# A list-scheduled attention and MLP kernel on one core: a recalibrated scheduler, other buffers and casts, and a new order of all engines

## The chip, the cores and the metric

The kernel runs on one core of a Trainium2 chip. The core has five engines with an instruction queue each: PE (TensorE, products; its weight loads are shown apart as PEld), DVE (VectorE), ACT (ScalarE), POOL (GpSimd) and SP (SyncE, which here only issues DMAs). Sixteen DMA engines move data between HBM and SBUF. The metric is the device time of one execution in microseconds. Each engine runs its own instructions strictly in their order; between engines, semaphores hold an instruction until what it needs is there.

## What is computed

Linear attention with positive features on 8 batches x 8 heads x 576 positions x 64 channels, then a layer norm and a two-layer MLP with a residual.

```python
def phi(x):                                        # 64 -> 256 features
    proj = np.einsum('bhsd,df->bhsf', x, w_phi)    # w_phi: 64 x 128
    proj = proj - np.max(np.abs(proj), axis=-1, keepdims=True)
    return np.concatenate([np.exp(proj), np.exp(-proj)], axis=-1)
q_p, k_p = phi(q), phi(k)
kv = np.einsum('bhsf,bhsd->bhfd', k_p, v); z = np.sum(k_p, axis=2)
attn = einsum(q_p, kv) / (einsum(q_p, z) + 1e-06)  # then heads joined: x is 8 x 576 x 512
xn = (x - mu) / np.sqrt(var + 1e-06) * g_ln
out = x + np.maximum(xn @ w_ch1, 0.0) @ w_ch2      # 512 -> 2048 -> 512
```

All inputs and the output are float32 in HBM.

## The kernel before

**Units and pairs.** The attention is cut into 32 units of 1152 rows, numbered n = 0 to 31. In pair 0 (units 0 to 7) a unit is two heads of one batch; in pairs 1 to 3 it is one head of two batches. Eight units make a pair, which is two whole batches, that is 9 tiles of 128 rows of `x`. A unit has eight full tiles of 128 rows and one mixed tile of the two leftovers of 64 rows.

**What a unit does.** `load_main` and `load_tails` bring k, q and v (the tails are `qx` and `vx`). q and k are turned so that channels lie on partitions: on PE for units 0 to 7 (`a_trans`, L470 and L478, copied out at L485 and L487), and by DMA from unit 8 on (`a_trans_dma`: two casts to bfloat16, a small one of 128 columns for the tails and a large one of 1024, at L536 on DVE, L538 on ACT or L540 on POOL; then one DMA transpose at L559 on SP's queue). PE makes the projections (L580, L581, L622, L628, L637), DVE the maxima (L584, L686), ACT the exponentials (L593, L597, L700, L754), POOL scales v by them (L712, L717, L721). PE sums over rows into `n_bank` (`a_kv`, L778 and L783), the result is copied to `KV` (L791 or L793), PE multiplies it by the query features (`a_num`, L829 and L835), DVE adds and inverts (L853, L859, L863), POOL puts the quotient into `x` (L869).

**What a pair does.** Once `x` is there, DVE takes statistics (L982, L996), DVE or ACT centers (L1000, L1005), and rows of 384 are turned into `xT` (on PE for pair 0, L946, by DMA for the others). For each of three blocks of 384 rows `moe` makes 16 groups of four products with w_ch1 (L1055, 128x384) and a relu (L1063, L1065), then 3 x 16 products with w_ch2 (L1122, 128x512; the last tile in halves, L1087), the scaled residual (L1130, L1135, L1141) and the store.

**Weights.** w_ch1 and w_ch2 are loaded in four quarters each from POOL's queue, with a cast to bfloat16 (L424, L435). w_ch1 is scaled by g_ln on DVE once pair 1 begins (L450, 16 instructions).

**What sets the order.** The whole order is made when the program is built. Each piece of work is an `Op` with an engine (or several, of which the first free one takes it), an assumed duration, what it reads and writes, and what buffers it acquires. `Order.run` walks through assumed time: each engine that is free takes the ready operation of lowest rank. The rank is the latest start that the end would allow, plus an offset from `OFF` by kind of work and by a table number (`stage_table`); `DUE` and `BLOCK` give the MLP's products due times. DMAs are modelled by two queues, `DMA` and `DMA_w` (those of POOL). A filler is a product of zeros into an unused part of `n_bank` (L1317, L1320); it is put on PE where PE has only operations that lack a buffer, up to the assumed time `WARM`. What `run` gives is emitted as a fixed order on each of the five engines; the assumed times themselves leave no wait behind, only the order does. Dependencies given as `came` (the gates of the weights) act in the assumed time alone.

```python
            late = min((latest[o.number] for o in op.users), default=1000.0) - op.lag
...
                if free[engine] > now + 1e-9 or not queue:
                    continue
...
                    if engine == self.filler[0] and now < self.filler[1]:
                        op = self.fill(now)
```

Of the kernel before, what the change touches and what calls it, by code (L numbers as in the profile page):

```python
# [10 lines left out]
FP32 = mybir.dt.float32  # L11
# [6 lines left out]
def bcast(ap: bass.AP, dim: int, n: int) -> bass.AP:  # L18
# [13 lines left out]
OFF = (  # L32
    {
        "load": 291.2, "trans": 30.0, "trans.copy": 30.0, "mixed": 49.3, "mixed.max": 23.2,
        "mixed.exp": 41.8, "k": 19.6, "k.max": 21.4, "k.em": -15.4, "k.exp": -46.8, "en": 15.6,
        "vv": -27.5, "q": 30.1, "q.max": 47.4, "q.em": 15.6, "tails": -42.2, "tails.exp": 7.3,
        "kv": -52.7, "kv.copy": 4.2, "num0": 51.4, "num1": -54.2, "num.dve": 32.4, "g1": 0.0,
        "g2": 0.0, "g3": 0.0, "put": -53.0, "ln": 201.7, "w1": -144.2, "w2": 207.3,
    },
    {  # L40
        "load": -11.5, "trans": -36.9, "trans.copy": 204.6, "mixed": 25.2, "mixed.max": -80.9,
        "mixed.exp": 132.7, "k": -79.5, "k.max": 146.3, "k.em": 53.6, "k.exp": -36.9,
# [4 lines left out]
    },  # L47
    {
        "load": 22.6, "trans": 17.7, "trans.copy": 96.2, "mixed": -96.6, "mixed.max": -70.2,
        "mixed.exp": -34.7, "k": -33.5, "k.max": -145.4, "k.em": -34.3, "k.exp": -84.1,  # L50
# [8 lines left out]
class Op:  # L59
    __slots__ = (  # L60
        "engines", "engine", "us", "emit", "rank", "lag", "deps", "users", "acquire", "release",
        "ready", "left", "number", "due",
# [9 lines left out]

class Order:


    def __init__(self, room):
        self.ops, self.wrote, self.read, self.room = [], {}, {}, dict(room)
        self.filler = (None, 0.0, 0.0, None)

    def add(self, engine, us, rank, emit, r=(), w=(), acquire=None, release=None, lag=0.2, due=None):  # L80
# [3 lines left out]
        op.engine, op.emit, op.rank, op.lag = None, emit, rank, lag  # L84
        op.acquire, op.release, op.due = acquire, release, due
# [14 lines left out]
    def fill(self, now):  # L100
        op = Op()
        op.engines, op.us, op.emit, op.rank = self.filler[:1], self.filler[2:3], self.filler[3], 0
        op.engine, op.lag, op.acquire, op.release = None, 0.0, None, None
        op.number, op.users, op.ready, op.left = -1, [], now, 0
        return op

    def run(self):
        waiting, free, room, events, done = {}, {}, self.room, [], []
        moving = {"DMA": 0.0, "DMA_w": 0.0}
# [19 lines left out]
        while events:  # L129
# [10 lines left out]
            for engine, queue in waiting.items():  # L140
                if free[engine] > now + 1e-9 or not queue:
                    continue
                passed = []
# [12 lines left out]
                if op is None:  # L156
                    if engine == self.filler[0] and now < self.filler[1]:
                        op = self.fill(now)
                    else:
                        continue  # L160
                op.engine = engine
# [3 lines left out]
                if isinstance(us, Move):  # L165
                    other = "DMA_w" if engine == "DMA" else "DMA"
                    moving[engine] = us.ns
                    turn = moving[other] + TURN if free.get(other, 0.0) > now else 0.0
                    us = us.packets * (us.ns + turn)
                elif isinstance(us, Op):  # L170
                    us = 1.1 if us.engine == "ACT" else 0.0
                end = now + us
# [19 lines left out]
def kernel(  # L192
# [37 lines left out]
    QB = 3  # L230
# [18 lines left out]
    nc.scalar.dma_start(out=wphi_f[D : 2 * D, :], in_=w_phi)  # L249
# [17 lines left out]

    wbk = consts.tile([P, 2, F], BF16, name="wbk")
    nc.vector.memset(wbk, 0.0)
    for i in range(2):  # L270
        rows = slice(i * D, (i + 1) * D)
# [8 lines left out]

    qk_bufs, v_bufs, vx_bufs = [], [], []
    for i in range(NBUF):
        qk_bufs.append(consts.tile([P, 2, HG, MX * D], FP32, name=f"qk{i}"))
        v_bufs.append(consts.tile([P, HG, MX * D], FP32, name=f"v{i}"))
    for i in range(2):

        vx = consts.tile([P, TG, 2, D1], FP32, name=f"vx{i}")
        nc.vector.memset(vx, 0.0)
        nc.vector.memset(vx[0:64, :, 0, D:D1], 1.0)
        nc.vector.memset(vx[64:128, :, 1, D:D1], 1.0)  # L290
        vx_bufs.append(vx)


    ea_bufs = []
    for i in range(2):
        eb = consts.tile([P, 2, (MX + 2) * P], BF16, name=f"ea{i}")
        nc.vector.memset(eb[:, :, MX * P :], 0.0)
        ea_bufs.append(eb)

    w1_sb = consts.tile([P, KC, DH], BF16, name="w1")  # L300
    w2_sb = consts.tile([P, JC, DM], BF16, name="w2")

# [7 lines left out]
    b16_bufs = [consts.tile([P, ST], BF16, name=f"b16_{i}") for i in range(2)]  # L310

# [1046 lines left out]
```

## Time and profile before

| what | value |
|---|---|
| time, median of 3 runs | 386.41 us (382.26, 386.41, 387.24) |
| the profiled execution | 381.13 us, span 379.3 us, granted clock 1.00 |
| busy of the span | PE 95%, DVE 67%, ACT 68%, POOL 54% |
| DMA | 53.31 MB, mean 141 GB/s; HBM read 36.77 MB, written 9.44 MB |
| chain that ended last | PE 62%, DVE 18%, DMA 8%, issue 5% |

The profile's times are of one execution, from its first to its last instruction; the time of a run holds a little more than that span. PE's busy time is the union of its instructions, each with its latency in the array, so an instruction can be shown at 326 ns where its successors follow every 162 ns. The chain of work that ended last cuts each piece to the time in which nothing else was waited for. "Idle before" names the instruction or DMA whose semaphore came last. In the slices each digit is the busy share of a fortieth of the span in tenths.

### The profile page before, as it was taken

To read this page: it belongs to the slowest core of one execution; us is meant where nothing else is said; L and a number is where in the kernel's file an instruction comes from. 1 tells how busy PE (TensorE), PEld (TensorE's weight loads), DVE (VectorE), ACT (ScalarE), POOL (GpSimd) and SP (SyncE) were. 2 spreads that over 40 slices of the span, in tenths; PEclk is the share of its full clock that TensorE was granted. 3 is DMA by queue.
4 is the path that set the end of the run, shared out by engine and by line. 5 is a ranking of instruction groups with operands and counts; after the bars stand their busy time and mean duration, and the time that the engine had idled before them with its cause. 6 is when DMAs were issued, how large, how long until landed. Compare 5 with 4: busy or idle time off the path is not lost.

```text
span 379.3 us, 9487 instructions
## 1 busy us (share of the span) xinstructions
PE 358.9 (95%) x3626; PEld 220.2 (58%) x3626; DVE 254.8 (67%) x557; ACT 257.9 (68%) x574; POOL 204.4 (54%) x350
## 2 busy tenths in 40 slices
PE   4999979988999999999999999999999999999995
PEld 2988856554656555556566555556565555555543
DVE  3698998988999999987787999787749000000001
ACT  3877898968787876896877878786746534444420
POOL 4787878847785768463967835572562101111031
PEclk9999999999999999999999999999999999999999
DMA  8999699999975499956664274430104230101012
GB/s 223 274 223 279 182 225 214 200 276 248 259 203 181 84 229 178 238 108 202 151 167 128 65 158 139 90 61 7 51 13 89 76 88 29 28 30 54 30 55 84
DMA packets 91133, 53.31 MB, mean 141 GB/s; under 512 B 57488, under 2 KB 86544, under 8 KB 91088
## 3 DMA queue, kind: packets, MB, share of 16 engines
q1 hardware_dynamic: 86000, 47.66, 50.5%
q0 software_dynamic: 4384, 4.46, 7.6%
q10 hardware_dynamic: 704, 0.59, 0.6%
q8 instruction: 28, 0.46, 0.5%
q14 instruction: 17, 0.14, 0.1%
HBM read 36.77 MB, written 9.44 MB: 122 GB/s over the span
## 4 chain that ended last, share of the span: by engine, by line
PE 62%; DVE 18%; DMA 8%; issue 5%; POOL 2%; ACT 2%; SPq 1%; DVEq 0%; POOLq 0%; ACTq 0%
PE hT_ps L1055 25%; PE ch_ps L1122 24%; DVE m L686 5%; DMA qkT<-b 5%; DMA qx<-in_k_dram 3%; PE n_bank L783 2%; DVE st L982 2%; PE pm L628 2%; DVE numc L853 2%; DVE numc L859 2%; PE num L829 2%; DMA xT<-xc 1%; DVE hT L1063 1%; PE pt L637 1%; ACT eb L700 1%
## 5 line engine op out<-in xcount | busy, mean ns | idle before, releaser
L1055 PE MATMUL hT_ps<-xT,w 128*128 128x384 bf16 x768 | 152.1, 326 | 1.9 <-DMA xT<-xc 0.8
L1122 PE MATMUL ch_ps<-w,hT 128*128 128x512 bf16 x560 | 150.2, 379 | 0.1
L1055 PEld LDWEIGHTS <-w 128*128 128x128 bf16 x768 | 71.8, 98 | 59.2 <-issue 4.0
L1065 ACT ACTIVATE hT<-hT_ps 128x384 bf16<-128x384 f32 x120 | 59.1, 492 | 56.9 <-PE hT_ps L1055 56.3
L686 DVE TENSOR_REDUCE m<-pm 128x8 f32<-128x1024 f32 x64 | 76.8, 1212 | 13.9 <-PE pm L628 9.7
L869 POOL TENSOR_TENSOR x<-numc,rden 128x384 bf16<-128x384 f32 (+3 forms) x88 | 45.9, 537 | 55.4 <-DVE rden L863 53.6
L1122 PEld LDWEIGHTS <-hT 128*128 128x128 bf16 x560 | 50.8, 98 | 41.4 <-issue 1.6
L700 ACT ACTIVATE eb<-pm 128x1024 bf16<-128x1024 f32 x64 | 65.1, 1038 | 6.3 <-DVE m L686 6.3
L754 ACT ACTIVATE ea<-pt 128x1024 bf16<-128x1024 f32 x64 | 63.6, 1029 | 5.9 <-PE pt L637 5.5
L1141 POOL TENSOR_TENSOR o<-o,x 128x512 f32<-128x512 f32 x20 | 23.1, 1155 | 75.4 <-ACT o L1135 75.4
L1130 DVE SCALAR_TENSOR_TENSOR o<-ch_ps,rstd,x 128x512 f32<-128x512 f32 x15 | 11.1, 741 | 56.7 <-PE ch_ps L1122 56.6
L712 POOL TENSOR_TENSOR vv<-v,em 128x512 bf16<-128x512 f32 x32 | 34.0, 1062 | 20.3 <-issue 15.9
L1063 DVE TENSOR_SCALAR hT<-hT_ps 128x384 bf16<-128x384 f32 x72 | 39.0, 547 | 8.1 <-PE hT_ps L1055 7.7
L712 POOL TENSOR_TENSOR vv<-v,en 128x512 bf16<-128x512 f32 x32 | 34.0, 1062 | 0.0
L829 PEld LDWEIGHTS <-ea 128*128 128x128 bf16 x512 | 23.6, 97 | 9.9 <-issue 3.1
L783 PE MATMUL n_bank<-vv,eb 128*128 128x65 bf16 x512 | 26.9, 194 | 0.0
L540 POOL TENSOR_TENSOR b<-qk,one 128x1024 bf16<-128x1024 f32 x11 | 20.8, 1895 | 10.4 <-DMA qkT<-b 7.2
L783 PEld LDWEIGHTS <-eb 128*128 128x128 bf16 x512 | 22.3, 98 | 3.7 <-issue 0.3
L982 DVE BATCH_NORM_STATS2 st<-x 128x6 f32<-128x512 bf16 (+1 forms) x44 | 24.4, 580 | 0.0
L853 DVE TENSOR_TENSOR numc<-num,em 128x390 f32<-128x390 f32 (+1 forms) x40 | 20.4, 517 | 5.6 <-PE num L829 3.9
L1320 PE MATMUL n_bank<-wz 128*128 128x120 bf16 x333 | 23.0, 221 | 1.2 <-DVE KV L791 0.8
L829 PE MATMUL num<-KV,ea 128*128 128x65 bf16 x416 | 19.7, 193 | 2.0 <-ACT xT L958 0.9
(91 smaller groups left out, 460.3 us busy)
## 6 DMA issues: line engine op xcount, KB each, us to landing
qk<-in_k_dram SPq DMA_DIRECT2D x32, 256.0 KB, 4.3
v<-in_v_dram SPq DMA_DIRECT2D x32, 256.0 KB, 5.6
out_dram<-o SPq DMA_DIRECT2D x31, 256.0 KB, 2.4
qk<-in_q_dram SPq DMA_DIRECT2D x30, 256.0 KB, 5.8
w<-in_moe_w_ch_dram POOLq DMA_DIRECT2D x8, 512.0 KB, 11.1
out_dram<-o SPq DMA_DIRECT2D x10, 128.0 KB, 2.4
qx<-in_k_dram SPq DMA_DIRECT2D x16, 64.0 KB, 4.8
qx<-in_q_dram SPq DMA_DIRECT2D x14, 64.0 KB, 3.5
```

Of the source, the lines that this page charges most:

```text
L686: nc.vector.reduce_max(out=m, in_=ps, axis=AX.X, apply_absolute_value=True)
L700: nc.scalar.activation(eb, ps, AF.Exp, scale=(1.0, -1.0)[t])
L712: nc.gpsimd.tensor_tensor(out=u["vv"][:, t, 0:MX, 0:D], in0=vb[:, hh, :].rearrange("p (c d) -> p c d", d=D), in1=bcast(e[:, 0:MX], 2, D), ...
L754: nc.scalar.activation(u["EA"][:, t, 0:1024], u["pt"], AF.Exp, scale=(1.0, -1.0)[t])
L783: nc.tensor.matmul(ps[:, t, c // 4, :], EB[:, t, c, :], vv[:, t, c, :], start=False, stop=(t == 0 and c == MX - 1), skip_group_check=True,)
L829: nc.tensor.matmul(ps[t][:, i, :], ea(u, t, c), KV[:, t, c // 4, :], start=True, stop=True,)
L869: nc.gpsimd.tensor_tensor(out=dst, in0=st["numc"][ps_, i : i + n, 0:D], in1=bcast(st["rden"][ps_, i : i + n], 2, D), op=ALU.mult,)
L982: nc.vector.bn_stats(out=pr["st"][:, t, half or 0, :], in_=x[:, t, h0 * D : h1 * D])
L1055: nc.tensor.matmul(st["ps"], w1_sb[:, kc, jj * P : (jj + 1) * P], xT_bufs[(pair * NR + r) % XB][:, kc::KC, :], start=(kc == 0), stop=(kc = ...
L1063: nc.vector.tensor_relu(h_sb, st["ps"])
L1065: nc.scalar.activation(h_sb, st["ps"], AF.Relu)
L1122: nc.tensor.matmul(ch[t], hT[r, jj][:, rt * P : (rt + 1) * P], w2_sb[:, jj, :], start=(jj == 0), stop=(jj == JC - 1),)
```

## The change

- **The scheduler's model.** A cast on DVE can be a `Port`: it also waits, in assumed time, for what POOL is doing (`port`), and POOL waits for it. DMA transposes take a `Turn` on SP that grows with what is queued. Lags and durations are set anew (`SLACK`, `LAND`, `LAND_T`, `LAND_W`); the first `COLD` us count PE as 1.9 times slower. The offsets `OFF` have ten tables instead of three: one for each of units 0 to 7, one for units 8 to 15, one for the rest. `DUE` and `BLOCK` change.
- **Fillers.** PE is filled also when no operation at all is ready, up to `WARM` = 75 instead of 45, and `FIRST` = 28 fillers stand ahead of everything. The zeros are written first of all on DVE.
- **Transposes.** Three units ahead instead of two (`AHEAD`), with four `qkT` buffers (`QB`) and three `b16` (`NB16`) instead of three and two.
- **Casts.** The small cast on DVE becomes a `tensor_reduce` with max over single elements. Of the large casts DVE has 10 instead of 4, ACT 5 instead of 9, POOL 9 instead of 11. Of the small ones DVE keeps 8, ACT has 9 instead of 7, POOL 7 instead of 9.
- **Weights.** The gates of w_ch1's quarters are loads of v of units 4 to 6 instead of k and v of unit 3; w_ch2 may follow w_ch1's second quarter instead of its last. On POOL's queue this gives w_ch1's quarters 1 and 2, then 0, w_ch2's quarters 3, 0, 1 and 2, then w_ch1's quarter 3. The loads of units 8 to 15 get a true semaphore wait for w_ch2's quarter 3 (`wait_for_w2`); it stands at the first of them on SP, and what follows on SP stands behind it.
- **Engines.** 8 of the 16 scalings of w_ch1 go to ACT, 2 of the centerings to POOL (`CENTER`); half of w_phi is loaded from POOL's queue instead of ACT's, and its copies go from POOL to DVE.
- `FOLD`, with its new branches (`folded`, `subtract`, `put_heads`, `put_row`), is 0: none of that code is in the program but one constant, `nident`.

The products on PE are the same in number and shape in both programs, but for the fillers: 334 and 614. In the diff the line numbers are those of each file.

```diff
-DUE = 30.89
-BLOCK = 115.16
-WARM = 45.0
-X_DMA, QK_DMA = 1, 8
+DUE = 27.47
+BLOCK = 17.68
+WARM = 75.0
+COLD, FIRST = 5.6, 28
+SLACK = ((0.22, 0.0, 0.0, 1.02), (0.35, 0.6, 1.6, 1.03))
+HOLD = 3
+X_DMA, QK_DMA, AHEAD = 1, 8, 3
-LAND, TURN = 1.7, 0.013
-GATE = (("k", 3), ("k", 3), ("v", 3), ("v", 3))
+FOLD = 0
+LAND, LAND_T, LAND_W, TURN, BARRIER = 2.8, 1.5, 3.0, 0.004, 0.4
+GATE = (("v", 4), ("v", 5), ("v", 5), ("v", 6))
...
+CENTER = ((("DVE", "ACT", "POOL"), (Port(0.27), 0.61, 1.2)), (("DVE", "ACT"), (Port(0.27), 0.61)))
...
-                if free[engine] > now + 1e-9 or not queue:
+                filling = engine == self.filler[0] and now < self.filler[1]
+                if free[engine] > now + 1e-9 or not (queue or filling):
                     continue
...
+                elif isinstance(us, Port):
+                    first, last = port[0], port[1]
+                    us = us.us + max(0.0, first - now if now < first else last - now)
+                    port[2] = now + us
+                elif isinstance(us, Turn):
+                    ahead = backlog["DMA"]
+                    if free["DMA_w"] > now:
+                        ahead *= 3.4
+                    us = max(us.us, max(0.0, free["DMA"] - now) + ahead - 0.5)
...
+                if engine == "POOL" and op.load is None:
+                    us += max(0.0, port[2] - now)
+                    port[0], port[1] = now + min(us, op.cut or us), now + us
+                if engine == "PE" and now < COLD:
+                    us *= 1.9
...
-    QB = 3
+    QB = 4
+    NB16 = 3
...
-    nc.scalar.dma_start(out=wphi_f[D : 2 * D, :], in_=w_phi)
+    nc.gpsimd.dma_start(out=wphi_f[D : 2 * D, :], in_=w_phi)
...
+    wz = consts.tile([P, P], BF16, name="wz")
+    nc.vector.memset(wz, 0.0)
...
-        nc.gpsimd.tensor_copy(out=wbk[rows, i, :], in_=wphi_f[rows, :])
+        nc.vector.tensor_copy(out=wbk[rows, i, :], in_=wphi_f[rows, :])
...
+    def wait_for_w2(load):
+        tc.add_manual_dep(
+            load.ins, w2_loads[HOLD].ins.name,
+            mybir.DependencyInfo(mybir.DependencyClass.Sync, mybir.DependencyReason.DATA),
+            reason="weights first",
+        )
...
-        dma("POOL", V, 1 << 20, emit, r=[("w1 came", NW - 1)], w=[("w2", n)], us=0.78, row=2048)
+        dma("POOL", V, 1 << 20, emit, r=[("w1 came", 1)], w=[("w2", n), ("w2 came", n)], us=0.78, row=2048)
...
-            add("DVE", 0.3, rank, lambda kc=kc: scale(kc), r=["gln"], w=[("w1", n, kc)])
+            add(("DVE", "ACT"), (Port(0.32), 0.62), rank, lambda e, kc=kc: scale(e, kc), r=["gln", "ngln"],
+                w=[("w1", n, kc)])
...
-            if engine == "DVE":
+            if engine == "DVE" and in_.shape[2] == D:
+                nc.vector.tensor_reduce(
+                    out=out, in_=in_.rearrange("p i (d one) -> p i d one", one=1), op=ALU.max,
+                    axis=AX.X,
+                )
+            elif engine == "DVE":
                 nc.vector.tensor_copy(out=out, in_=in_)
...
-        add(("DVE", "ACT", "POOL"), (0.6, 1.02, 2.1), rank, cast_main, r=[*loaded(u, "q"), *loaded(u, "k")],
-            w=[("b16", n % 2)])
+        add(("DVE", "ACT", "POOL"), (Port(0.6), 0.98, 1.87), rank, cast_main, r=[*loaded(u, "q"), *loaded(u, "k")],
+            w=[("b16", n % NB16)])
...
     def stage_table(n):
-        return (n >= H // 2) + (n >= H)
+        return min(n, H) + (n >= 2 * H)
...
-            a_trans_dma(units[QK_DMA])
-        if QK_DMA <= n + 2 < NU and n + 2 > QK_DMA:
-            a_trans_dma(units[n + 2])
+            for m in range(QK_DMA, QK_DMA + AHEAD - 1):
+                a_trans_dma(units[m])
+        if QK_DMA + AHEAD - 1 <= n + AHEAD < NU:
+            a_trans_dma(units[n + AHEAD])
...
-                    x_center(pr, t, V)
+                    x_center(pr, t, rk("ln.c", n - 1))
...
-                            x_trans_dma(pr, t // NM, V)
+                            x_trans_dma(pr, t // NM, rk("ln.t", n - 1))
...
+    for _ in range(FIRST):
+        fill()
     sched.filler = ("PE", WARM, mm(1, WN), fill)
```

More of the change, by code (lines that the diff above doesn't have):

```diff
@@ L403, in load_tails @@
             )
-            issue(queue, rank, dst, src, [(key + "x" + str(half), j)], 16384 * TG, row=256)
+            issue(
+                queue, rank, dst, src, [(key + "x" + str(half), j)], 16384 * TG,
+                row=4096 if queue == "POOL" else 256, hold=HOLD >= 0 and H <= n < 2 * H, n=n,
+            )
     def loaded(u, key):
@@ L800, in a_kv, with move_rows, move @@
             r=[("EB", 0, n % 2), ("EBx", n % 2), ("vv", 0, n % 2)], w=[("kv", n)])
-        add(("ACT", "DVE"), (0.31, 0.35), rk("kv.copy", n), copy, r=[("kv", n)], w=[("KV", n % 3)], release=("N", 1))
+        add(("ACT", "DVE"), (0.28, 0.35), rk("kv.copy", n), copy, r=[("kv", n)], w=[("KV", n % 3)], release=("N", 1))
+    def move_rows(u, b, V):
+        half = 1 - b
+        rows = slice(half * 64, half * 64 + 64)
+        def move():
+            nc.sync.dma_start(
+                out=u["x"][b * 64 : b * 64 + 64, MX, :].rearrange(
+                    "p (i two d) -> p i two d", two=2, d=D
+                )[:, :, half, :],
+                in_=xs[rows],
+            )
+        dma("SP", V, 32768, move, row=128, r=[("xs", b, j) for j in range(4)],
+            w=[("x", 0, 2, 2 * j + half) for j in range(4)])
     def a_num(u, part):
@@ L815, in products @@
             KV = u["KV"]
-            if part:
+            if part and not folded(n):
                 ps = n_bank if pair else ps_B.tile([P, 512], FP32, tag="B", name="num")
@@ L825, in products @@
             st["ps"] = ps
+            if folded(n):
+                for i, c in enumerate((3, 7, MX, MX) if part else cs):
+                    for t in range(2):
+                        nc.tensor.matmul(
+                            ps[0][:, i, :], u["EX"][:, t, 1, :] if c == MX else ea(u, t, c),
+                            KV[:, t, i - 2 if c == MX else c // 4, :], start=(t == 0), stop=(t == 1),
+                        )
+                return
             for t in range(2):
@@ L925, in a_num @@
                     if i == 3:
[L926 to L935 removed]
+                        move_rows(u, b, V)
     def x_trans(pr, kc, r, V):
```

427 lines of the change are left out of this document (312 added, 115 removed), and 8 rows, old and new, of the table OFF.

## The prediction

> **What bounds the kernel now.** I read the page first, for the shares and the forty slices.
>
> ```profile
> span 379.3 us, 9487 instructions
> ...
> PE 358.9 (95%) x3626; PEld 220.2 (58%) x3626; DVE 254.8 (67%) x557; ACT 257.9 (68%) x574; POOL 204.4 (54%) x350
> ...
> PE   4999979988999999999999999999999999999995
> ...
> DVE  3698998988999999987787999787749000000001
> ...
> DMA  8999699999975499956664274430104230101012
> ```
>
> TensorE (PE) is the bound almost everywhere; only the first fifth has slices of it under 9, and there VectorE (DVE) and the DMA engines are as full as it is. So I cut the span into stages; behind each stage and its length stand the busy time and, in brackets, the instructions of PE, its weight loads, DVE, ACT and POOL, then PE's granted clock, the DMA share and GB/s.
>
> ```profile
> 0.00:14.80 14.80, 9.06 (x82) 6.74 (x83) 6.32 (x23) 7.72 (x16) 7.23 (x18) 1.00 0.91 243
> 14.80:50.00 35.20, 33.36 (x650) 30.70 (x648) 32.59 (x73) 28.66 (x65) 30.09 (x64) 1.00 1.04 231
> 50.00:70.00 20.00, 16.11 (x200) 10.19 (x200) 18.55 (x42) 18.09 (x42) 16.21 (x40) 1.00 1.25 225
> 70.00:160.00 90.00, 85.44 (x913) 50.26 (x911) 83.73 (x180) 69.73 (x159) 61.27 (x96) 1.00 0.90 211
> 160.00:300.00 140.00, 139.80 (x1378) 82.04 (x1377) 110.37 (x239) 103.47 (x236) 79.17 (x127) 1.00 0.41 102
> 300.00:375.20 75.20, 75.13 (x414) 40.23 (x411) 2.77 (x5) 30.28 (x59) 10.39 (x9) 1.00 0.15 48
> ```
>
> From 160 on PE idles 0.27 us in 215; nothing can be won there. "Busy" does not mean useful, though: up to 50 us many of PE's instructions are fillers, products of zeros. The groups by form give the counts, and the chain, which cuts each piece to its own share, gives the pace.
>
> ```profile
> L1055 PE MATMUL hT_ps<-xT,w 128*128 128x384 bf16 x768 | 152.1, 326 | 1.9 <-DMA xT<-xc 0.8 <-DVE numc L859 0.8 <-DVE numc L853 0.3
> L1122 PE MATMUL ch_ps<-w,hT 128*128 128x512 bf16 x560 | 150.2, 379 | 0.1
> L1320 PE MATMUL n_bank<-wz 128*128 128x120 bf16 x333 | 23.0, 221 | 1.2 <-DVE KV L791 0.8 <-ACT KV L793 0.5
> ```
>
> ```profile
> 9.64 1.92 PE n_bank L1320 x20
> 24.25 0.94 PE n_bank L1320 x18
> 56.43 0.26 PE n_bank L783 x8
> 56.69 1.95 PE hT_ps L1055 x12
> 100.39 0.37 PE num L829 x12
> 369.91 1.73 PE ch_ps L1122 x8
> 371.64 3.51 PE ch_ps L1087 x32
> ```
>
> A filler takes 0.94/18 = 0.052 us, an L1055 product 1.95/12 = 0.1625, an L1122 product 1.73/8 = 0.216. Useful work is the same before and after, instruction for instruction: 768 x 0.1625 = 124.8, 560 x 0.216 = 121.0, the 32 half-width ones 3.5, and attention 76.4 (kv 512 x 0.0325 + 64 x 0.055, num 640 x 0.031, the projections by the starts of the rows below, the 108 transposes at the 0.055 of L581): **325.7 us**. The span of before is thus 325.7 useful, 333 x 0.0525 = 17.5 filler, 379.3 - 375.15 = 4.15 behind the last product, and some 32 of waiting, a cold start among it. Those 49.5 us are all that a new order can touch.
>
> ```profile
> 68.40 0.39 PE L637 MATMUL pt<-qkT,wbk 64*128 64x512 bf16 x2
> 68.63 0.39 PE L628 MATMUL pm<-wbk,qkT 64*128 64x128 bf16 x8
> 68.95 0.82 PE L1055 MATMUL hT_ps<-xT,w 128*128 128x384 bf16 x4
> 69.79 0.27 PE L580 MATMUL n_bank<-wbk,qkT 128*128 128x256 bf16 x1
> 69.90 0.22 PE L581 MATMUL n_bank<-qkT,wbk 128*128 128x128 bf16 x1
> 69.95 2.86 PE L1055 MATMUL hT_ps<-xT,w 128*128 128x384 bf16 x16
> ```
>
> This stretch is the yardstick. In the old order 32.55 us of useful work stand ahead of the sixteen products at 69.95.
>
> **The change, part by part.** The two built programs differ on PE in one count alone: 614 fillers for 334. The new list fills whenever PE would stand (the old one only when some operation lacked a buffer), and until 75 us instead of 45.
>
> *Up to the last filler.* In the new order 33.85 us of useful work and all 614 fillers, 32.2 us, stand up to there; PE cannot be earlier than their sum. It starts sooner.
>
> ```profile
> PE n_bank L1317 <- DVE wz L1316: 3.4, 1, 3.4
> ...
> DVE wbk L269 <- PEq L1342: 0.8, 1, 0.8
> ```
>
> The zeros that PE waits for until 3.4 become the first thing that DVE writes, at 0.8: a start at 1.0. It starts cold: twenty fillers took 1.92 at 9.64 against 0.94 for eighteen later, so some 46 cold instructions cost 2.0 more. Sum: 1.0 + 2.0 + 32.2 + 33.85 = **69.1**. Before had the same useful work behind it at 69.95 + 8 x 0.1625 = **71.25**. So the fillers leave 2.1 us to win. What the new order loses again when data come later than the list thought lies between 0 and 5% of 66 us (1.84 idle of 35.20 in the second stage), 3.5; I take 1.5, nearer to 0, because part of the old idle is of the kind now filled. DVE does not move this: its work ahead of the seventeenth main maximum is 51 us in the old order and 53 in the new, by the same durations.
>
> The second half of w_phi goes to POOL's queue and the copies of it from POOL to DVE. The nearest load from that queue lands in 4.1 us.
>
> ```profile
> qx<-in_q_dram POOLq DMA_DIRECT2D x2, 64.0 KB, 4.1
> ```
>
> Issued first, by 2 us, that is about 6.5 with the copy; the first projection now stands behind 57 cold fillers and transposes, near 7. Hidden; if not, up to 1 us at the start, inside the 1.5.
>
> *From there to 280 us.* Before needs 375.15 - 71.25 = 303.9 for the remaining 291.85: it loses **12.05**. Of this 4.8 is idle shown in the stages (90.00 - 85.44, and 0.20); the other 7.3 are waits shorter than a product's latency, and errors of my paces. What makes them:
>
> ```profile
> 72.96 7.50 DMA qkT<-b
> ...
> 83.91 4.44 DMA qx<-in_k_dram
> 88.35 5.11 DMA qkT<-b
> ```
>
> ```profile
> L536 DVE CAST b<-qx x8: 217/456/1869, 49.3 to 237.5; 128x128 bf16<-128x128 f32 x8
> L536 DVE CAST b<-qk x4: 680/691/1235, 93.8 to 200.7; 128x1024 bf16<-128x1024 f32 x4
> ```
>
> The transposes by DMA are issued two units ahead and come late; the change issues them three ahead (a fourth qkT buffer, a third b16). A small cast takes 217 ns or up to 1869: 8 x (746 - 217) = 4.2 us of DVE standing, in a stage where DVE is 93% busy. As maxima they cost between the bare 217 and the 416 of a maximum over 256 columns; that gives back 2.6 to 4.2 of DVE. The Trainium skill says why: "SBUF — State Buffer", "Who interferes with whom", has casts able to take the ports shared with GpSimd, and a tensor_reduce on trn2 never; by that page the whole 4.2 would go. The trace agrees that such casts vary; no row here shows a reduce that reads SBUF.
>
> Against it: six more large casts on DVE, 6 x 0.69 = 4.1; eight scalings of w_ch1 go from DVE to ACT (about 4 us, ACT is 77% busy there); two centerings go to POOL. These even out, so DVE's total stays. What the stage can give back is 0 to 7.2 (the 4.8, and a third of the 7.3, as the rest also holds my own errors). I take 4.7: the lateness of two transposes and half of the casts. Then 7.35 stay.
>
> *w_ch1 behind v, and the hold.* The first weight quarter now needed comes third, the four quarters of w_ch2 follow it at once, and SP waits for the first of these before loading units 8 to 11.
>
> ```profile
> L424 POOL DMA_DIRECT2D w<-in_moe_w_ch_dram x4: 750/777/800, 15.5 to 19.3; - x4
> ...
> DMA to landing us min/median/max: 8.8/13.2/16.9
> ```
>
> ```profile
> 26.61 0.29 POOL L869 TENSOR_TENSOR xs<-numc,rden 64x64 bf16<-64x64 f32 x1
> ```
>
> ```profile
> 40.01 1.07 SPq L347 DMA_DIRECT2D qk<-in_k_dram  x2
> ```
>
> POOL stands at that place at 26.6 in before, so the awaited quarter is issued near 28 and lands between 37 and 45; before reaches those loads at 40.0. Between 3 us won and 5 lost; I take nothing, the middle. Behind SP's wait stand four units of loads and the first transposes.
>
> **Sum**: 69.1 + 1.5 + 291.85 + 7.35 + 4.15 = 373.95 of span; the profiled run had 1.83 around its span (381.13 - 379.30): **375.8**, against 381.13. But that run is the quickest of four (382.26, 386.41, 387.24); its median lies 5.3 higher. I give the changed kernel half of that, as earlier transposes should take up some of what varies: **378**.
>
> **The rivals.** *The waits return*: the 12.05 stay, and data come 3.5 late in the first stage: 69.1 + 3.5 + 291.85 + 12.05 + 4.15 + 1.83 = 382.5, with the old spread up to 388. For it: DVE stays at 93% between 70 and 160. Against: two of the three long pieces of the chain are transposes that now start earlier. *Everything is won*: no lateness, 7.2 given back: 371.8 to 373. *Slower*: the hold. Four quarters took 36.2 - 15.5 = 20.7 us to land in before; now five stand in one row, with units 6 and 7 beside them. If the awaited one lands at 57 instead of 40, pair 1 is 17 late, its layer norm too, and PE runs out of pair 0's products: 375.8 + 17 = 393, 395 with some spread. It decides from 45 on, us for us. Against: that quarter is the second of the five. *The change does not do what it says*: the wait sits on one quarter only, so the rest still mix with the loads; that is the first rival.
>
> **How the numbers follow.** Forecast (373 to 382) 0.58, waits return 0.25, everything won 0.08, slower 0.09. The range 371 to 388 leaves out the hold. Two per cent, about what a measurement of this kernel can tell from no change, lie at 378.7 and 394.1: faster is the best case and two thirds of the forecast, 0.46; slower is the hold, 0.08 without its cases just under the line; the rest 0.46.
>
> **What would show it.** Right: the first product near 1 us; sixteen L1055 products around 70 as now; PE's idle between 70 and 160 down from 4.56 to about 2; small casts gone from DVE, each maximum under 0.42; SP issuing unit 8's loads by 45. Wrong: PE waiting among the fillers by more than 3.5 in all, SP standing behind w_ch2 past 50, or idle of 4 and more left between 70 and 160.

## The result, and the profile after

| | before | changed |
|---|---|---|
| median of 20 runs each | 383.52 us (378.8 to 387.24) | **387.75 us** (384.7 to 391.7) |
| profiled execution | 381.13, span 379.3 | 384.93, span 383.1 |

The ratio is **1.0136, 95% interval [1.0114, 1.0159]**: slower, by less than 2% and by far more than its uncertainty. 378 with a range of 371 to 388 was forecast: the time stands just inside the range, and its direction was forecast wrong. Both pairs in the table differ by about the same, 4.2 and 3.8, so the profiled executions may be set against each other.

The page of the changed kernel, its totals, slices and chain:

```profile
span 383.1 us, 10019 instructions
...
PE 370.8 (97%) x3906; PEld 235.6 (62%) x3906; DVE 250.6 (65%) x548; ACT 262.1 (68%) x588; POOL 203.3 (53%) x347
...
PE   8969999899999999999999999999999999999995
...
PE 88%; DMA 6%; ACT 2%; POOL 1%; issue 1%; DVE 0%; SPq 0%; ACTq 0%; POOLq 0%; DVEq 0%
```

Its stages, with the columns as in the prediction:

```profile
0.00:14.80 14.80, 13.56 (x200) 12.79 (x201) 8.01 (x27) 8.12 (x15) 7.93 (x19) 1.00 0.94 247
14.80:50.00 35.20, 30.71 (x558) 27.88 (x555) 26.38 (x60) 24.85 (x62) 26.31 (x57) 0.95 1.16 224
50.00:70.00 20.00, 20.00 (x333) 16.42 (x331) 18.06 (x43) 17.32 (x35) 15.71 (x34) 1.00 0.91 191
70.00:160.00 90.00, 87.94 (x970) 53.99 (x970) 81.36 (x174) 75.01 (x173) 62.96 (x102) 1.00 0.88 214
160.00:300.00 140.00, 140.00 (x1425) 82.55 (x1424) 112.53 (x242) 105.04 (x246) 79.97 (x129) 1.00 0.45 104
```

From 70 on all is as forecast: idle of 2.06 between 70 and 160, where before had 4.56. Of the 2.06, 1.39 lie ahead of the last filler, which stands at 80.03; behind it PE idles for 0.67 us up to 160, where before idled for 4.56 behind the same work. The start is as forecast as well, 13.56 busy for 9.06. But in the second stage PE stands for 4.49 us, where before stood for 1.84; DVE does 26.38 us of work for 32.59, and the granted clock falls to 0.95. PE's waits name what it stood for (line waited for, us in total, times, longest):

```profile
PE qkT_ps L613 <- DMA qk<-in_q_dram: 1.7, 1, 1.7
PE qkT_ps L613 <- DMA qk<-in_k_dram: 1.6, 1, 1.6
PE n_bank L1584 <- DVE wz L376: 1.0, 1, 1.0
PE n_bank L1587 <- ACT ea L755: 0.9, 1, 0.9
```

The timeline of PE at that place, and at the last fillers and products (start, us, line and operation, count, the wait before it; L613 is the transpose of q and k, L1587 the filler):

```profile
19.59 0.27 PE L1587 MATMUL n_bank<-wz 128*128 128x120 bf16 x2
21.45 0.40 PE L613 MATMUL qkT_ps<-ident,qk 128*128 128x128 bf16 x4 [1.60 <-DMA qk<-in_k_dram]
23.59 0.40 PE L613 MATMUL qkT_ps<-ident,qk 128*128 128x128 bf16 x4 [1.74 <-DMA qk<-in_q_dram]
23.82 1.38 PE L1587 MATMUL n_bank<-wz 128*128 128x120 bf16 x20
25.95 1.06 PE L801 MATMUL pm<-wbk,qkT 128*128 128x256 bf16 x4
...
29.41 0.60 PE L801 MATMUL pm<-wbk,qkT 128*128 128x256 bf16 x4
...
30.59 0.69 PE L1587 MATMUL n_bank<-wz 128*128 128x120 bf16 x10 [0.52 <-DVE KV L991]
...
79.87 0.32 PE L1587 MATMUL n_bank<-wz 128*128 128x120 bf16 x3
...
374.92 3.66 PE L1351 MATMUL ch_ps<-w,hT 128*128 128x256 bf16 x32
```

PE is ready for unit 4's k at 19.85 and has it at 21.45; it gets q at 23.59. Right behind this its work is slow: the four projections at 25.95 take 1.06, in the same timeline those at 29.41 take 0.60. The last fillers stand at 80, not at 70.6.

Before did not meet this. It comes to the same transposes only at 23.64, and had issued the loads earlier:

```profile
23.64 0.61 PE L470 MATMUL qkT_ps<-ident,qk 128*128 128x128 bf16 x8
```

```profile
13.71 0.43 SPq L347 DMA_DIRECT2D qk<-in_k_dram  x1
14.46 0.37 SPq L347 DMA_DIRECT2D qk<-in_q_dram  x1
```

The same issues in the changed kernel, on SP's queue and on POOL's:

```profile
8.92 1.32 SPq L469 DMA_DIRECT2D v<-in_v_dram  x2
11.09 1.78 SPq L469 DMA_DIRECT2D qx<-in_k_dram  x2
13.01 1.67 SPq L469 DMA_DIRECT2D qx<-in_q_dram  x2
14.85 0.48 SPq L469 DMA_DIRECT2D qk<-in_k_dram  x1
15.68 0.37 SPq L469 DMA_DIRECT2D qk<-in_q_dram  x1
```

```profile
14.48 1.54 POOL L561 DMA_DIRECT2D w<-in_moe_w_ch_dram  x2
```

Unit 4's k and q stand behind unit 5's v and four tails, and two quarters of w_ch1 are issued on POOL 0.4 us ahead of them. So the new order asks for these data 3.8 us earlier than before (19.85 for 23.64) and issues them 1.1 and 1.2 us later. Before loads w_ch1 at this place, too, but issues its four quarters from 15.49 on, behind unit 4's k and q; these took 4.6 and 5.8 us to land there, and 6.6 and 7.9 in the changed kernel.

### The profile page after: what moved, and what is told of

Read it like the earlier page. It is cut to its first block, busy times and chain, and to the rows that moved or that the text cites. A ratio compares the mean times of both kernels' runs of the same rounds, so it can differ in the third digit from the quotient of the medians.

```text
span 383.1 us, 10019 instructions
## 1 busy us (share of the span) xinstructions
PE 370.8 (97%) x3906; PEld 235.6 (62%) x3906; DVE 250.6 (65%) x548; ACT 262.1 (68%) x588; POOL 203.3 (53%) x347
## 3 DMA queue, kind: packets, MB, share of 16 engines
q0 software_dynamic: 4416, 4.49, 7.2%
## 4 chain that ended last, share of the span: by engine, by line
PE 88%; DMA 6%; ACT 2%; POOL 1%; issue 1%; DVE 0%; SPq 0%; ACTq 0%; POOLq 0%; DVEq 0%
PE hT_ps L1319 32%; PE ch_ps L1386 31%; PE n_bank L1587 6%; DMA qk<-in_q_dram 4%; PE n_bank L983 4%; PE pm L807 4%; PE num L1054 3%; PE pt L816 2%; DMA qx<-in_k_dram 2%; PE n_bank L977 1%; PE n_bank L1054 1%; PE ch_ps L1351 1%; PE n_bank L1060 1%; PE n_bank L729 1%; ACT ea L951 1%
## 5 line engine op out<-in xcount | busy, mean ns | idle before, releaser
L1386 PE MATMUL ch_ps<-w,hT 128*128 128x512 bf16 x560 | 148.1, 379 | 0.1
L1329 ACT ACTIVATE hT<-hT_ps 128x384 bf16<-128x384 f32 x125 | 61.5, 493 | 69.2 <-PE hT_ps L1319 68.8
L1098 POOL TENSOR_TENSOR x<-numc,rden 128x192 bf16<-128x192 f32 (+3 forms) x88 | 46.8, 546 | 52.6 <-DVE rden L1090 50.5
L1587 PE MATMUL n_bank<-wz 128*128 128x120 bf16 x613 | 43.4, 222 | 2.5 <-ACT ea L755 0.9
L1327 DVE TENSOR_SCALAR hT<-hT_ps 128x384 bf16<-128x384 f32 x67 | 37.0, 553 | 11.9 <-PE hT_ps L1319 11.4
L1587 PEld LDWEIGHTS <-wz 128*128 128x128 bf16 x613 | 36.7, 101 | 4.9 <-issue 3.4
L1054 PEld LDWEIGHTS <-ea 128*128 128x128 bf16 x512 | 24.5, 98 | 6.9 <-issue 0.7
L1084 DVE TENSOR_TENSOR numc<-numc,num 128x390 f32<-128x390 f32 (+1 forms) x40 | 20.6, 517 | 0.5
```

Source lines behind the costliest of these rows:

```text
L1054: nc.tensor.matmul(ps[t][:, i, :], ea(u, t, c), KV[:, t, c // 4, :], start=True, stop=True,)
L1098: nc.gpsimd.tensor_tensor(out=dst, in0=st["numc"][ps_, i : i + n, 0:D], in1=bcast(st["rden"][ps_, i : i + n], 2, D), op=ALU.mult,)
L1327: nc.vector.tensor_relu(h_sb, st["ps"])
L1329: nc.scalar.activation(h_sb, st["ps"], AF.Relu)
L1386: nc.tensor.matmul(ch[t], hT[r, jj][:, rt * P : (rt + 1) * P], w2_sb[:, jj, :], start=(jj == 0), stop=(jj == JC - 1),)
L1587: nc.tensor.matmul(warm, wz, wz[:, 0:WN], start=False, stop=False, skip_group_check=True)
```

## The experiments

The theory after the result, **A1**: w_ch1's quarters share the DMA engines with unit 4's loads and make them late. **A2**: the loads' own place on SP's queue does. **B**: the fillers, now 614, stand on the path. **C**: without them the clock falls. Where a run moves or leaves out something, the finished list `done` is edited ahead of its emission, so that the rest of the order stays.

**The two quarters put off.** Two issues on POOL move from 14.5 us to just ahead of the negation of g_ln, which POOL reaches at 23.5.

```diff
+        ahead_of([("w1", 1), ("w1", 2)], "ngln")
         for op in done:
             if op.emit and len(op.engines) > 1:
```

> The changed kernel, with the loads of w_ch1's quarters 1 and 2 moved on POOL's queue from 14.5 us to behind unit 2's scaling of v, at about 25 us; the other engines' orders are the same. Theory A1 (unit 4's q and k came late because two quarters of the weights shared the DMA engines with them): they land by 21 us, PE's wait of 3.3 us falls under 1, the slow clock behind it goes, and the kernel takes 382 to 384. Theory A2 (they came late because they stand late on SP's queue): the wait stays over 2.5 us and the gain is under 1 us.

Measured: **381.56 us** (380.87 to 383.96), ratio to before 0.9937 [0.9898, 0.9977]: 6.2 less than the changed kernel, and less than before. Its PE timeline at the same place, and its second stage:

```profile
20.67 0.40 PE L622 MATMUL qkT_ps<-ident,qk 128*128 128x128 bf16 x4 [0.19 <-DVE qkT L637]
21.40 0.40 PE L622 MATMUL qkT_ps<-ident,qk 128*128 128x128 bf16 x4 [0.34 <-DMA qk<-in_q_dram]
...
26.80 0.69 PE L1596 MATMUL n_bank<-wz 128*128 128x120 bf16 x10 [0.52 <-DVE KV L1000]
...
76.09 0.32 PE L1596 MATMUL n_bank<-wz 128*128 128x120 bf16 x3
...
371.14 3.66 PE L1360 MATMUL ch_ps<-w,hT 128*128 128x256 bf16 x32
```

```profile
14.80:50.00 35.20, 33.52 (x654) 30.82 (x652) 30.53 (x71) 29.09 (x69) 30.41 (x67) 1.00 1.11 226
```

The waits are down from 1.60 and 1.74 us to 0.19 and 0.34: 2.19 us won at q (23.59 - 21.40). From there to the fillers behind KV it needs 5.40 us for the changed kernel's 7.00, the same instructions: 1.6 won by the clock. The sum, 3.79, is still there at the last fillers (79.87 - 76.09) and at the last products (374.92 - 371.14). Nothing in between gives any of it back: PE's waits from there to the last fillers are the same four in both traces (0.52, 0.46, 0.52 and 0.87 us), only 3.8 us apart. The medians differ by 2.4 more than these two executions. The profiled execution of the changed kernel was one of its quickest: its granted clock was 0.996, the median of its 20 runs is 0.9905, and this difference is some 2 us of 386 (an estimate). With the quarters put off the two clocks are 0.997 and 0.998.

What the DMA engines did from 14 to 26 us, in the changed kernel first and then with the quarters put off (queue, packets, MB, share; issues, KB each, median us to landing):

```profile
q1 hardware_dynamic: 2821, 1.93, 63.2%
q0 software_dynamic: 1049, 1.04, 53.0%
...
qk<-in_k_dram SPq DMA_DIRECT2D x4, 256.0 KB, 8.1
qk<-in_q_dram SPq DMA_DIRECT2D x4, 256.0 KB, 8.5
```

```profile
q1 hardware_dynamic: 4428, 3.09, 90.8%
...
qk<-in_k_dram SPq DMA_DIRECT2D x4, 256.0 KB, 4.3
qk<-in_q_dram SPq DMA_DIRECT2D x4, 256.0 KB, 4.3
```

A k or q lands after 4.3 us without w_ch1 beside it and after 8.1 or 8.5 with it. Unit 4's own take 4.2 and 4.0 us here, although SP issues them at 16.38 and 17.39, later than in the changed kernel. The Trainium skill, "DMA: Bandwidth & Descriptors", "Queues, rings and completion order", says that each DMA engine goes round the queues that have work, packet by packet. The trace fits this, though it was read by queue and not by packet: SP's queue moves 1.93 MB in 12 us with POOL's beside it and 3.09 MB without.

**Unit 4's loads first** (A2), with w_ch1 where the change has it.

```diff
+        ahead_of([("k", 4), ("q", 4)], ("v", 5))
```

> The changed kernel, with the loads of unit 4's k and q put ahead of unit 5's v and the four tails on SP's queue; the other engines' orders are the same. Theory A2 (place on SP's queue): they are issued near 9 us instead of 14.85 and 15.68, land by 17, PE's wait for them goes, and the kernel takes 382 to 384. Theory A1 (the weights' share of the DMA engines): also on time, since they come before the weights; but what is moved back, unit 5's v and the tails, comes late in turn, the wait moves there and the gain is under 2 us.

Measured: **389.1 us**, 1.0112 [1.0061, 1.0162], no different from the changed kernel. The first of PE's waits:

```profile
PE qxT_ps L630 <- DMA qx<-in_q_dram: 6.4, 1, 6.4
```

The loads put behind now come late. The order on SP decides which unit's data starve, the bytes beside them that something does: A1 stands, A2 falls.

**No hold.** SP's wait for w_ch2 is left out, the order stays.

```diff
             load = eng.dma_start(out=dst, in_=src)
-            if hold:
-                wait_for_w2(load)
```

> The changed kernel (387.75 us) without the real wait of SP's first tail of unit 8 for w_ch2's last quarter; the order of everything is the same. Theory A (the hold costs nothing, since unit 8's data are needed only after 65 us and SP is free by 56 us): within 1.5 us of 387.75. Theory B (rival 4 of the prediction: SP's standing sets unit 8's start): TensorE reaches unit 8's projections by 67 us instead of 70, 383 to 386 us.

Measured: **387.64 us**, 1.0107 [1.0069, 1.0146]. In the changed kernel SP stands from 39.5 to 48.77; without the hold it stands to 49.11, because the move of `xs` into `x` ahead of unit 8's loads waits for POOL anyway. PE reaches unit 8's sixteen projections at 70.44 for 70.09. The hold costs nothing that shows: it ended at 38.92, as the awaited quarter landed, and PE waits for no load but unit 4's in the changed kernel.

**The small casts as casts again.**

```diff
-            if engine == "DVE" and in_.shape[2] == D:
+            if False:
```

> The changed kernel, with the eight small casts on VectorE as plain copies again; the orders are the same. The casts stand behind 49 us. If the maxima are what they were costed at, VectorE loses 2.6 to 4.2 us of standing again between 70 and 240 us, PE's idle in 70 to 160 grows by up to 1 us, and the time by 0 to 1.5 us (387.75 to 389). If the maxima themselves cost, the time falls below 387.

Measured: **389.25 us**, 1.0118 [1.0049, 1.0187]. That can't be told from the changed kernel. The tile `b` on DVE, as maxima in the changed kernel and then as casts in this one (duration in ns min/median/max, first and last start):

```profile
L679 DVE TENSOR_REDUCE b<-qx x8: 248/276/278, 59.8 to 210.8; 128x128 bf16<-128x128 f32 x8
```

```profile
L684 DVE CAST b<-qx x8: 209/916/2140, 62.8 to 214.4; 128x128 bf16<-128x128 f32 x8
```

Eight maxima never took more than 278 ns; the casts went up to 2140. "Who interferes with whom" in "SBUF — State Buffer" of the Trainium skill says that a tensor_reduce on trn2 never takes the ports shared with GpSimd. The eight, none above 278 ns, agree. DVE gets 5.8 us back (8.0 for 2.2 busy, by the groups), but the end does not show it, within an interval of 2.7 us either way.

**Fillers cut, with w_ch1 where the change has it.** The last 422 are left out. They are products of zeros that nothing reads.

```diff
+        fillers = [o for o in done if o.tag == "filler"]
+        for o in fillers[163:]:
+            o.emit = None
```

> The changed kernel in its own order, but the last 422 of its 614 fillers, all that stand behind the transposes of unit 4 that came late, are not put on PE; nothing else differs. Theory A (the delay is kept): PE lost 3.3 us waiting for unit 4's q and k and some 2.3 us of slow clock behind it, and the fillers, which stand in the fixed order, keep PE from catching up. Then the point of the last filler, at 80.0 us in the changed kernel, comes at 72 to 75, and the kernel takes 380 to 383 us instead of 387.75. Theory B (the chain): VectorE, ScalarE and the loads set the pace of the first 80 us, and the fillers only lie in what would be idle; then the time stays within 1 us of 387.75. Theory C (the clock): without fillers PE's clock falls between 24 and 80 us, PEclk well under 1 there, and the kernel gets slower than 388.

Measured: **385.07 us**, 1.0031 [0.9996, 1.0065]: 2.7 won, less than the 5 to 8 of A, as part of C came true. Its second and third stage:

```profile
14.80:50.00 35.20, 24.17 (x349) 19.58 (x347) 26.50 (x61) 25.48 (x63) 25.67 (x56) 0.80 1.16 228
50.00:70.00 20.00, 16.71 (x184) 11.05 (x184) 17.95 (x40) 16.34 (x35) 15.08 (x32) 0.75 0.77 196
```

The granted clock is 0.80 and 0.75 in the mean of 55 us, and waits for loads of unit 4's time are still there (2.3 for a tail of q at 22.39, 1.8 for k at 24.56), with a new one of 2.9 for a q at 75.21.

**Fillers cut, with the quarters put off**: the last 170 left out, then every second one behind the first 163, then both.

```diff
+        for o in fillers[-170:]:
+            o.emit = None
```

> The changed kernel with w_ch1's two quarters put off (e2_w1_later, 381.56 us), and its last 170 fillers (the ones planned after about 50 us) left out; output the same. Theory A: once nothing waits for loads, the first part is bound by TensorE's fixed stream, where the fillers are as much work as the products: 170 x 0.0525 = 8.9 us leave it, of which the vector work gives back 3 to 8 us, so 374 to 379 us, the granted clock staying at 0.99 or more (before had no filler after 50 us and 1.00 there). Theory B: the arrival of the vector results sets the pace and a filler only stands in a gap: within 1.5 us of 381.6. Theory C: the clock falls below 0.98 and the gain is lost: 381 us or more with a clock below 1.00 between 50 and 80 us.

```diff
+        for o in fillers[163::2]:
+            o.emit = None
```

> The changed kernel with w_ch1's two quarters put off (e2_w1_later, 381.56 us), and every second filler after the first 163 planned ones left out (some 225 of 614, 11.8 us of TensorE); output the same. Theory A (fillers bound the first part): 4 to 9 us faster, 372 to 378 us, clock 0.99 or more. Theory C (the clock needs them): TensorE waits in small pieces and the granted clock falls below 0.98 between 15 and 70 us as with all of them cut, so 380 us or more.

```diff
+        for o in fillers[163:-170:2] + fillers[-170:]:
+            o.emit = None
```

> e5_e2_late_fillers (380.08 us) with every second of the fillers between the first 163 and the last 170 left out too, so about 330 of 614 stand. Theory A (in the stretch up to 40 us fillers are still on the path, so what two cuts win adds up): 378.0 to 379.6 us. Theory B (vector results set the pace there, as halving alone won only 0.4 us): within 1 us of 380.1. Theory C (the clock needs them): clock below 0.98, over 381 us.

Measured: **380.08** (0.9907 [0.9866, 0.9947]), **381.14** (0.9929 [0.9901, 0.9956]) and **380.64 us** (0.9897 [0.9846, 0.9949]). The cuts take out 170, 211 and 296 fillers, 8.9, 11.1 and 15.5 us, and win up to 1.5, with intervals that overlap that of the quarters put off alone: what they leave is taken up by waits. Two stages of the second of them, the third stage of the first and of the last, and the waits of the first between 50 and 80 us:

```profile
14.80:50.00 35.20, 29.16 (x524) 24.59 (x522) 31.17 (x71) 29.41 (x70) 30.94 (x69) 1.00 1.13 226
50.00:70.00 20.00, 17.29 (x260) 12.95 (x258) 18.77 (x40) 16.09 (x33) 12.96 (x27) 1.00 0.97 233
```

```profile
50.00:70.00 20.00, 14.21 (x190) 9.24 (x190) 18.73 (x43) 16.32 (x35) 13.38 (x29) 0.96 1.06 226
```

```profile
50.00:70.00 20.00, 15.15 (x187) 9.63 (x188) 17.96 (x40) 14.65 (x28) 13.55 (x29) 0.91 0.92 217
```

```profile
PE pm L819 <- ACT eb L895: 2.9, 1, 2.9
PE n_bank L989 <- POOL vv L916: 1.3, 2, 0.8
```

With every second filler PE stands for 6.04 us of the second stage and the clock is 1.00; DVE has 31.17 us of work in it, hardly more than the 30.53 with all fillers and the quarters put off, where PE stands for 1.68. So once the loads come in time, the vector results allow hardly more than the fillers do, and most fillers stand in a gap: theory B of the first and the last of these, not A. The time that C gave for the second came as well (380 us or more), but not its clock. In the other two the clock did fall, for 3.4 us at half speed each, which is up to 1.7 us of work; up to that much of what these cuts won may be lost again to the clock.

**Both moves of loads**, without and with those cuts of fillers.

```diff
+        ahead_of([("w1", 1), ("w1", 2)], "ngln")
+        ahead_of([("k", 4), ("q", 4)], ("v", 5))
```

> The changed kernel with both moves: w_ch1's two quarters put off, and unit 4's k and q loaded ahead of unit 5's v and four tails. Theory A (with w_ch1 gone, what is left of the first part's lateness before 21 us is the place of unit 4's loads on SP's queue: TensorE, VectorE and ScalarE all wait there for them): 379 to 381 us, and unit 4's transposes by 20 us in place of 20.7 to 21.4. Theory B (the DMA engines move what they can either way, a load put first makes another one late): within 1 us of e2_w1_later's 381.56 or slower, with TensorE waiting for tails of q or k in the place of unit 4's q.

> The same with e10_e5_half_mid's filler cuts (380.64 us): if unit 4's loads are what carries the chain up to 22 us, 377 to 379.5 us; if a load put first makes another one late, within 1 us of 380.6 or slower.

Measured: **381.73** (0.9988 [0.9959, 1.0018]) and **380.65 us** (0.9954 [0.9926, 0.9981]). Theory B both times: with unit 4's k and q first, PE waits 0.9 and 0.7 us for a tail of q instead, and in the first of the two the last fillers stand at 76.04 for 76.09. Before's own median was 382.85 beside these runs and 383.93 beside the one with the quarters put off alone, so by the ratios, too, the second move wins nothing.

**The list without the ports**, and **with before's depth of transposes**, each with the quarters put off; here the list is laid out anew.

```diff
-                    us = us.us + max(0.0, first - now if now < first else last - now)
+                    us = us.us
...
-                    us += max(0.0, port[2] - now)
+                    us += 0.0
```

> The changed kernel with w_ch1's two quarters put off (381.56 us), and the list laid out without the ports: no time is added to a GpSimd operation beside a vector one or the other way round, all else as in the change, so only the order of work is another. Theory A (the second part's gain comes from the order that counts the ports): its loss rises from about 7 to 10 to 12 us, 384 to 387 us. Theory B (the gain comes from the number of units' buffers and loads ahead, or any order found would do): within 1.5 us of 381.6.

```diff
-X_DMA, QK_DMA, AHEAD = 1, 8, 3
+X_DMA, QK_DMA, AHEAD = 1, 8, 2
...
-    QB = 4
-    NB16 = 3
+    QB = 3
+    NB16 = 2
```

> The changed kernel with w_ch1's two quarters put off (381.56 us), and with before's depth of the transposes: two units ahead in place of three, three buffers of the transposed q and k in place of four, two of the cast ones in place of three. The list is laid out anew with that, its offsets stay, so the order differs too. Theory A (my prediction: the second part's gain of about 5 us comes from transposes that start earlier): TensorE's idle time from 70 to 160 us rises from 1.5 to 5 us or more, 385 to 388 us. Theory B (the order that counts the ports gave it, not the depth): within 2 us of 381.6.

Measured: **391.04** (1.0189 [1.0108, 1.027]) and **403.28 us** (1.05 [1.0438, 1.0563]), 9.5 and 21.7 more than with the quarters put off alone. That looks like a price for both, so two controls followed, in which a constant of the list changes, and on the chip nothing but the list that comes out (the order, which engine takes a piece, and 616 and 644 fillers for 614).

```diff
-CENTER = ((("DVE", "ACT", "POOL"), (Port(0.27), 0.61, 1.2)), (("DVE", "ACT"), (Port(0.27), 0.61)))
+CENTER = ((("DVE", "ACT", "POOL"), (Port(0.30), 0.61, 1.2)), (("DVE", "ACT"), (Port(0.30), 0.61)))
```

> A control for the two runs in which the list was laid out anew. The changed kernel with w_ch1's two quarters put off (381.56 us), ports counted, all loads, buffers and depths kept; only the list's own time for a vector centring is 0.30 in place of 0.27, an edit without a meaning for the chip, after which another order comes out with the same offsets. Theory A (counting the ports, and the depth, are what the second part's gain rests on, so their losses of 9.5 and 21.7 us are theirs): within 2 us of 381.6. Theory B (the offsets fit one list only, and any other list laid out with them loses): 4 us or more slower, 386 to 400, so that those two runs don't price the ports or the depth.

```diff
-LAND, LAND_T, LAND_W, TURN, BARRIER = 2.8, 1.5, 3.0, 0.004, 0.4
+LAND, LAND_T, LAND_W, TURN, BARRIER = 2.6, 1.5, 3.0, 0.004, 0.4
```

> A second control of that kind: the changed kernel with w_ch1's two quarters put off (381.56 us), the list's time for a load's landing 2.6 in place of 2.8, all else kept. Theory A: within 2 us of 381.6. Theory B: 386 to 400.

Measured: **391.45** (1.0223 [1.0195, 1.025]) and **395.26 us** (1.0323 [1.0287, 1.036]). An edit without a meaning costs 9.9 or 13.7 us. The stage from 70 to 160 us of the first control:

```profile
70.00:160.00 90.00, 82.72 (x870) 49.78 (x868) 69.36 (x152) 71.93 (x164) 63.46 (x97) 0.97 0.84 204
```

Idle of 7.3 where the changed kernel has 2.06. The offsets fit one list, and another list laid out with them loses. So those two runs price neither the ports nor the depth: the 9.5 are no more than what a list that the offsets don't fit costs, and of the 21.7 no share can be told from it. Which part of the change the second part's gain comes from stays open.

## Why the prediction was wrong

Against its sum, in the terms of the profiled execution (375.8 forecast, 384.93 measured):

| step | forecast | measured |
|---|---|---|
| first product | 1.0 | wait of 1.0, right |
| up to the last filler | 69.1 + 1.5 late | 80.0: **9.4 more** |
| from there to the last product | 291.85 + 7.35 = 299.2 | 374.92 + 3.66 - 80.0 = 298.6: right |
| behind it | 4.15 | 383.1 - 378.6 = 4.5 |
| around the span | 1.83 | 384.93 - 383.1 = 1.83 |
| median over the profiled run | 2.6 | 387.75 - 384.93 = 2.8 |

**The step that failed is the lateness of the first part, 1.5 with bounds of 0 and 3.5.** It measured 10.9. PE idled for 6.1 us of this beyond its start, 3.3 of them for unit 4's k and q; more than 3.5 was the prediction's own sign of being wrong. I bounded the lateness by the idle share of before's second stage. That share was of an order which comes to unit 4 at 23.64. The new order starts PE 2.4 us sooner and comes to unit 4 at 19.85, but its data had been asked for later, and behind w_ch1 instead of ahead of it. A start that is won on PE is worth something only where the loads can follow, and the DMA engines had no room: the prediction's own row of 14.8 to 50 us has them at a share of 1.04, which I read past. I weighed "w_ch1 behind v" only as the hold at 40 us, not for what its first two quarters do at 14.5.

Of the 10.9, **3.8 are w_ch1's two quarters**: 2.2 of waiting and 1.6 of slower clock behind it, shown by the run that puts them off. Of the 7.1 left in that run (76.2 for 69.1), the stages show 3.5 of PE's idle time beyond the start, 2.4 of it in four waits for results of DVE and ACT. By the starts of the products in that trace, the same waits hold some 1.5 more that lie within the latency of the product ahead, and the useful work took some 35.7 us, not the 33.85 of my paces (both are estimates). Cutting fillers, in three runs, and moving unit 4's loads, in two, won back 1.5 at most; what would win the rest stays open.

**The fillers.** I took PE's fixed stream for the bound of this part. In the changed kernel PE carries the chain behind the wait, and what is lost stays lost. But 8.9 to 15.5 us less of it win at most 1.5, so the vector results are nearly as late as the fillers; "DVE does not move this" was too simple.

**The second part** came as forecast: idle of 2.06 for "about 2", 298.6 for 299.2. The runs don't show why. I had named the deeper transposes and the casts. The casts gave DVE 5.8 us for the 2.6 to 4.2 forecast, and the end did not show it; the depth could not be priced by itself. A sum that comes out right is no evidence for the causes it was made of.

**The hold.** The awaited quarter landed by 38.92, between the 37 and 45 forecast, and SP issued the first of unit 8's loads there; the others began at 49.45, not by 45. PE shows no wait for them, though the rival had this place decide from 45 on, us for us. What stood there was the move of `xs`, not the hold. **w_phi** was hidden: the first projection came at 5.75, where 7 was forecast. **The rivals**: "the waits return" had its time right (382.5 to 388) but only half of its place: its 3.5 of lateness in the first part came, and far more, while the second part's waits went. **The spread** of half of 5.3 was right in size (2.8 for 2.6) for the wrong reason: before's own median came down to 383.52 in 20 runs, and in the changed kernel the time goes with the granted clock, 0.997 and 0.996 in its two quickest runs (384.70 and 384.93) and 0.9905 in the median.

## What to carry to other kernels

When an engine is made to start earlier, ask next who feeds it: write beside each early consumer when its load is issued, what is ahead of it on its queue, and what other queue shares the DMA engines then. Weights that are needed some 40 us later (the first product with w_ch1 starts at 56.38) can cost more by their place than by their bytes; here two issues moved by 9 us turned a loss of 1.4% into a gain of 0.6%, and with a cut of fillers it was 0.9% (380.08 us, the lowest median here, which the intervals don't tell from the 0.6%). And a list made with fitted offsets can't be ablated by laying it out anew: edit the finished order, or run a control that changes nothing of meaning.

## What the runs showed of the hardware

The clock fell after less waiting than I had expected, and not always after more. Two waits of 1.60 and 1.74 us, 0.4 us of work between them, were followed by a granted clock of 0.69:

```profile
20.00:25.00 5.00, 1.81 (x29) 1.64 (x30) 0.71 (x2) 2.94 (x7) 4.62 (x10) 0.97 1.17 246
25.00:30.00 5.00, 5.00 (x63) 4.26 (x62) 3.13 (x5) 1.40 (x2) 1.54 (x3) 0.69 1.14 302
```

With 422 fillers cut, it was 0.75 from 50 to 70 us, though no wait of PE from 30 to 60 us was above 1.2 us; with every second one cut it was 1.00 at a PE that idled for 17% of the second stage. The Trainium skill, "TensorE: Matmul & The Clock Gate", "Part 1: The HAM clock gate (the "warmup" mystery)", gives half clock after an idle window of about 3.4 us, and tells of a kernel in which PE idles so often for a moment that the clock swings between half and full. The first pair of waits, 3.3 us in 3.7, is near to that window; the stretch at 0.75 has no such window, and there the measurement decides.

What tells these runs apart is how much of a stretch of 3.41 us PE was busy. In the traces' record of the clock it is 1.00 or 0.50, and it changes only in steps of 3.41 us from its first rise: in the changed kernel up at 4.25, half from 24.73 to 28.14. Ahead of the first rise (11.34 before) the rows print 1.00, though the twenty fillers at 9.64 ran at half their pace.

| kernel | stretch, us | PE busy in it, us | clock in the next stretch |
|---|---|---|---|
| changed | 17.91 to 21.32 | 1.95 (57%) | 1.00 |
| changed | 21.32 to 24.73 | 1.54 (45%) | 0.50 |
| 422 fillers cut | 32.85 to 36.27 | 1.78 (52%) | 0.50 |
| 422 fillers cut | 46.51 to 49.92 | 1.82 (53%) | 0.50 |
| every second filler cut, its emptiest | 48.30 to 51.71 | 2.15 (63%) | 1.00 |

In the sixteen traces of this case, the clock fell after 17 of the stretches at full clock. PE was busy for under 45% in nine stretches, and the clock fell after all nine; it fell after 8 of the 17 with 45 to 60%, and after none with more. What decides between 45 and 60% stays open.
